# A new hand-written order of steps, with the same code

## The chip, the cores and the metric

The kernel runs on one core of a Trainium2 chip. The metric is the device time of one execution in microseconds. The core has five engines that run side by side, each with its own instruction stream in order: PE (TensorE: matmuls; its weight loads are listed as PEld), DVE (VectorE), ACT (ScalarE), POOL (GpSimd, which here mostly issues loads) and SP (SyncE, which here issues the writes of the result). They wait for one another by semaphores.

## The reference

```python
def _attn_ref(q, k, v, p):                       # q, k, v: 8 x 8 x 576 x 64, p: 8 x 8 x 32 x 64
    scale = 1.0 / np.sqrt(q.shape[-1])
    def sm_attn(qq, kk, vv):
        s = scale * np.matmul(qq, kk.transpose(0, 1, 3, 2))
        s = s - np.max(s, axis=-1, keepdims=True)
        a = np.exp(s)
        a = a / (np.sum(a, axis=-1, keepdims=True) + 1e-09)
        return np.matmul(a, vv)
    p_packed = sm_attn(p, k, v)
    return sm_attn(q, p_packed, p_packed)

# x: attention's output as 4608 tokens x 512;  w_in: 512 x 2048;  w_out: 2048 x 512
h = x @ w_in
r = np.maximum(h, 0.0)
out = (r * r) @ w_out
```

There are two attentions in a row: 32 packed rows attend to 576 keys, then 576 queries attend to the 32 results. After them comes a feed-forward layer with a squared relu.

## The kernel before

The work is cut by batch (8), by quad of four heads (2 in a batch), by half of a batch's 576 tokens (256 and 320 in batches 0 and 1, 288 and 288 after them), by block of 128 of the 2048 hidden columns (16, paired to 8), and by tile of 128 output rows (36). The second attention's product with `p_packed` isn't formed: `p_packed` is multiplied by w_in first (`wp`), so that layer 1 is the matmul of `wp` with the transposed weights `a2T`.

What runs when stands in one string, `ORDER`. Its words are steps, and `run` calls `step` for each in turn. Each step gives its instructions to one engine or two, so the words of one engine, in order, are that engine's instruction stream. A word's suffix names the engine where there is a choice: `:v` is DVE, `:a` is ACT, `:p` is POOL. A buffer is taken where the word that fills it stands, from those whose last reader stands earlier in the string.

The words, with batch b, quad n, half f, block i, pair j, tile t:

| words | step | engine |
|---|---|---|
| Lkbn, Lvbn, Lqb, LA/LB; Wi, Wo; Pr | loads of k, v, q (LA and LB are the parts of q of batches 0 and 1); of w_in and w_out in pieces; of the rest of p | POOL's queue |
| pf; P0, P1 | load of p of batches 0 and 1 (three DMAs into one tile); scaling and transposing it | SP; DVE |
| I | the identity matrix | POOL |
| Zn.m | n idle matmuls of 512 columns and m of 256 (L338); nobody uses their result | PE |
| kTbn; s1b; m1, x1 | transpose of k (L354); scores of the first attention; maximum, exponential | DVE; PE; DVE, ACT |
| eT, eo; pv, pp | transpose of the exponentials on PE and its copy; product with v and its scaling | PE, any; PE, DVE |
| pt, po; bd, bs | two transposes of pp and their copies | PE, any; DVE, any |
| QA, QB, EA, EB (batch 0); qA, qB, qT | transpose of q, on PE with a copy, or on DVE (L366) | PE, any; DVE |
| zA, zB, s2 | scores of the second attention (A and B are the halves in batches 0 and 1) | PE |
| t, m, s, x, u, a, T with A or B; t2, m2, sb, x2, su, a2, aT | softmax of it and the transpose to `a2T` | DVE, x on ACT, some on POOL |
| wa, wb, w0, w1; Wa, Wb, W0, W1 | `wp` in pieces of columns (L609); its copy out of PSUM (L452, L454) | PE; ACT or DVE |
| hb.f.i; rb.f.i; qb.f.j | layer 1 (L625); relu (L630 on ACT, L632 on DVE); square into `gT` (L668 on ACT, L670 on DVE) | PE; ACT or DVE; any |
| ot.j; ct; dt | two of a tile's 16 matmuls of layer 2 (L683); copy out of PSUM; write to DRAM (L714) | PE; ACT or DVE; SP |

PSUM holds two banks for tiles of `h` in batch 1 and after (`y`; in batch 0 two for even and two for odd blocks), two for tiles of `o` (`x`), and two double banks for the rest (`psa`). SBUF holds three buffers for k, two for q, three for v from batch 2 on, and five for a copied output tile (`o_sb`).

Of the kernel before, what the change touches and what calls it, by code (L numbers as in the profile page):

```python
# [70 lines left out]
qT21 q1.1.3:a o4.6 h1.1.12 r1.1.0:a bd2 pt2 qT20 o4.7 bs2:a Lk40 h1.1.5 po2:v r1.1.12:a o5.7 q1.1.0:v c4:a h1.1.10
r1.1.5:v c5:a s22 d4 r1.1.10:v h1.1.4 o6.0 t221 r1.1.4:a h1.1.9 d5 o7.0 q1.1.2:a t220 h1.1.13 r1.1.9:a o6.1 qT30
r1.1.13:a Lq4 h1.1.11 q1.1.4:a m221 w120 w121 r1.1.11:a o6.2 m220 W121:a h1.1.14 h1.1.15 W120:v Lv31 o6.3 r1.1.14:a
q1.1.6:a o7.1 o6.4 sb21:v r1.1.15:a Lv40 o7.2 q1.1.5:a kT30 o7.3 q1.1.7:a o7.4 sb20:v Lk41 x221 o6.5 qT31 o7.5 x220 o6.6
su21 o6.7 o7.6 su20 c6:a o7.7 w020 a221:v c7:a d6 w021 o8.0 W020:a a220:v o8.1 d7 o8.2 aT21 W021:a o8.3 aT20 o8.4 Lq5
h2.0.1 h2.0.0 r2.0.1:v o8.5 r2.0.0:a o8.6 q2.0.0:v h2.0.2 h2.0.3 r2.0.2:v o9.0 Lk50 o8.7 r2.0.3:v h2.0.5 c8:a s13
q2.0.1:v r2.0.5:a h2.0.4 d8 m130 o10.0 r2.0.4:a h2.0.6 kT40 h2.0.7 r2.0.6:a o10.1 r2.0.7:a q2.0.2:v h2.0.10 Lk51 x130
m131 o9.1 h2.0.8 r2.0.10:a q2.0.3:v o9.2 r2.0.8:a kT41 h2.0.13 x131 eT30 h2.0.9 r2.0.13:v o10.2 eo30:a rd3 r2.0.9:v
h2.1.1 eT31 q2.0.4:v h2.0.14 r2.1.1:a o10.3 r2.0.14:v eo31:a h2.0.11 Lk61 o9.3 r2.0.11:v o9.4 h2.0.12 h2.1.5 q2.0.5:v
r2.0.12:a pv3 r2.1.5:v h2.0.15 q2.0.6:v h2.1.4 pp3 r2.0.15:a o9.5 r2.1.4:v h2.1.6 bd3 pt3 q2.0.7:v h2.1.0 bs3:a o9.6  # L80
r2.1.6:v r2.1.0:v Lv41 po3:a o9.7 q2.1.2:v h2.1.8 q2.1.0:v c9:a h2.1.2 r2.1.8:v s23 r2.1.2:a Lv50 d9 o11.0 t230 h2.1.3
h2.1.7 t231 o10.4 r2.1.3:a w130 m230 r2.1.7:a w030 W130:a h2.1.10 q2.1.1:v h2.1.9 q2.1.3:v o10.5 W030:a m231 o10.6 o11.1
sb30:v r2.1.10:a o11.2 r2.1.9:a sb31:v o10.7 x230 o11.3 q2.1.4:v c10:a h2.1.15 qT40 o11.4 x231 h2.1.11 su30 r2.1.15:a
w031 d10 r2.1.11:a w131 W031:a h2.1.14 su31 h2.1.13 o12.0 r2.1.14:a a230:v o12.1 r2.1.13:a o12.2 W131:a q2.1.5:v o12.3
a231:v h2.1.12 o11.5 aT30 r2.1.12:a o12.4 aT31 o12.5 q2.1.6:v q2.1.7:v h3.0.5 h3.0.2 qT41 r3.0.5:a o12.6 h3.0.0 r3.0.2:v
Lq6 o11.6 r3.0.0:a o12.7 h3.0.1 h3.1.1 r3.0.1:v c12:a o11.7 r3.1.1:v s14 d12 c11:a q3.0.0:v h3.0.4 kT50 h3.0.3 r3.0.4:a
o13.0 r3.0.3:a m140 d11 h3.0.9 Lk60 o14.0 r3.0.9:a q3.0.1:v h3.1.3 x140 kT51 h3.1.0 o14.1 r3.1.3:a m141 o13.1 Lk70
r3.1.0:a h3.0.8 q3.0.2:v eT40 x141 h3.0.7 r3.0.8:v o13.2 eo40:v r3.0.7:a h3.0.6 q3.1.0:v o14.2 q3.0.4:v r3.0.6:a eT41
rd4 q3.0.3:v h3.0.11 eo41:a h3.1.2 r3.0.11:v o14.3 r3.1.2:v o13.3 h3.0.12 h3.0.10 q3.1.1:v pv4 r3.0.10:a r3.0.12:v o14.4
Lv51 pp4 h3.0.13 q3.0.5:v h3.0.14 r3.0.13:a bd4 o13.4 r3.0.14:v bs4:a pt4 Lv60 q3.0.6:v h3.0.15 h3.1.8 o13.5 po4:v  # L90
r3.1.8:a o14.5 r3.0.15:v s24 q3.0.7:v h3.1.11 t240 h3.1.6 r3.1.11:a o13.6 t241 r3.1.6:a o13.7 w040 qT51 c13:a w041
h3.1.4 W040:a m241 o16.0 d13 h3.1.5 m240 r3.1.4:a o16.1 r3.1.5:a o14.6 W041:a sb41:v h3.1.9 h3.1.7 q3.1.2:v o14.7
r3.1.7:a sb40:v r3.1.9:a w140 w141 x241 q3.1.3:v h3.1.10 c14:v o16.2 W141:a h3.1.13 q3.1.4:v d14 o15.0 su41 r3.1.10:a
o16.3 x240 o15.1 r3.1.13:v W140:a h3.1.12 q3.1.5:v o16.4 a241:v o15.2 r3.1.12:a h3.1.14 su40 h3.1.15 o16.5 r3.1.14:a
q3.1.6:v o15.3 r3.1.15:a a240:v o15.4 o16.6 q3.1.7:v o15.5 aT40 aT41 o16.7 qT50 o15.6 c16:a h4.0.1 h4.0.4 Lq7 r4.0.1:v
o15.7 d16 r4.0.4:v o17.0 c15:a h4.0.3 h4.0.2 r4.0.3:v o17.1 r4.0.2:a d15 s15 q4.0.1:v h4.0.0 kT60 h4.0.9 o17.2 r4.0.0:a
m151 o17.3 r4.0.9:a h4.0.6 m150 o17.4 r4.0.6:a h4.1.3 q4.0.0:v x151 o17.5 kT61 o18.0 x150 o17.6 r4.1.3:v Lk71 h4.0.5
h4.0.13 rd5 r4.0.5:a o18.1 r4.0.13:v eT50 h4.0.11 eo50:v h4.0.12 eT51 q4.0.2:v o17.7 r4.0.12:v r4.0.11:a o18.2 eo51:a
c17:v h4.1.2 h4.0.10 q4.0.6:v r4.1.2:a pv5 d17 r4.0.10:a h4.0.7 Lv61 q4.1.1:v h4.0.15 r4.0.7:a o19.0 q4.0.5:v r4.0.15:a
pp5 o19.1 q4.0.3:v o19.2 Lv71 bd5 h4.0.8 pt5 bs5:v h4.1.11 r4.0.8:a o18.3 po5:v q4.0.4:v h4.1.1 s25 r4.1.11:a r4.1.1:v  # L100
# [761 lines left out]
```

## Time and profile before

| | |
|---|---|
| time, median of 3 runs (lowest, highest) | 241.13 us (241.06, 241.85) |
| the profiled execution: its own time, its span | 242.64 us, 240.8 us |
| PE busy | 228.9 us, 95% of the span |
| DVE busy | 201.4 us, 84% |
| ACT busy | 144.2 us, 60% |
| POOL busy | 73.4 us, 30% |
| granted TensorE clock | 1.0 |

The span reaches from the first to the last instruction that was profiled; the execution's own time has the start and the end around it. A line of a group reads: line of the code, engine, operation, what it writes and reads, shapes, count, then busy time in us and the mean of one in ns, then the idle time of the engine just before. A line of the timeline reads: start and duration in us, engine, line, operation, tiles, shapes, count, and in brackets how long the engine stood idle before it and what ended that. A line of DMA issues ends with the size of one and the time from issue to landing. Some matmul records are missing from a trace.

### The profile page before, as it was taken

How to read it: one execution, taken by the hardware profiler on the slowest of the kernel's cores; microseconds unless marked ns; L12 is line 12 of the kernel's file. 1: busy time of each engine (PE TensorE's matmuls, PEld its weight loads, DVE VectorE, ACT ScalarE, POOL GpSimd, SP SyncE). 2: the span in 40 equal slices, each digit the busy share in tenths (PEclk: the TensorE clock that was granted, in tenths of full speed). 3: DMA queues.
4: the chain of work that ended last, by engine and by line, in shares of the span. 5: the costliest groups of instructions: out<-in, count | busy, mean ns of one | idle time of the engine just before them, and what ended most of it. 6: DMA issues, size and time to landing. Idle time of an engine off the chain costs nothing.

```text
span 240.8 us, 6042 instructions
## 1 busy us (share of the span) xinstructions
PE 228.9 (95%) x2373; PEld 124.6 (52%) x2408; DVE 201.4 (84%) x456; ACT 144.2 (60%) x311; POOL 73.4 (30%) x122
## 2 busy tenths in 40 slices
...
GB/s 108 177 197 209 187 197 206 172 239 195 197 194 211 177 169 144 44 78 211 110 79 37 196 125 52 59 37 102 39 23 73 49 46 44 44 41 49 46 63 112
DMA packets 33404, 28.51 MB, mean 118 GB/s; under 512 B 8160, under 2 KB 28384, under 8 KB 33376
## 3 DMA queue, kind: packets, MB, share of 16 engines
...
q1 hardware_dynamic: 6384, 9.51, 14.7%
...
## 4 chain that ended last, share of the span: by engine, by line
PE 83%; DVE 7%; DMA 4%; issue 2%; POOL 1%; SPq 1%; ACT 1%; POOLq 0%
PE ps_o L683 48%; PE ps_h L625 25%; DMA gT<-in_v_dram 4%; PE ps_wp L609 3%; PE ps_s L408 3%; PE ps_e1T L466 2%; PE ps_pv L490 1%; SPq L714 1%; DMA out_dram<-o_sb 1%; DVE gT L670 1%; DVE mx L558 1%; DVE d L564 1%; DVE r L632 1%; DVE sums L576 1%; ACT qT L452 1%
## 5 line engine op out<-in xcount | busy, mean ns | idle before, releaser
L683 PE MATMUL ps_o<-w_out_bf,gT 128*128 128x512 bf16 (+1 forms) x544 | 140.9, 378 | 2.0 <-issue 0.5
L625 PE MATMUL ps_h<-a2T,wp 128*128 128x288 bf16 (+2 forms) x512 | 89.9, 286 | 1.4 <-DVE wp L454 0.6
L630 ACT ACTIVATE r<-ps_h 128x288 bf16<-128x288 f32 (+2 forms) x161 | 61.4, 413 | 48.8 <-PE ps_h L625 43.2
L683 PEld LDWEIGHTS <-gT 128*128 128x128 bf16 x576 | 54.6, 98 | 43.6 <-issue 3.4
L625 PEld LDWEIGHTS <-wp 128*128 128x128 bf16 x512 | 47.4, 98 | 41.9 <-issue 7.4
L632 DVE TENSOR_SCALAR r<-ps_h 128x288 bf16<-128x288 f32 (+2 forms) x95 | 41.3, 449 | 11.3 <-PE ps_h L625 10.6
L670 DVE TENSOR_TENSOR gT<-r 128x576 bf16<-128x576 bf16 (+2 forms) x108 | 46.5, 444 | 2.1 <-ACT r L630 1.2
L452 ACT CAST wp<-ps_wp 128x1024 bf16<-128x1024 f32 (+1 forms) x31 | 29.1, 962 | 8.8 <-PE ps_wp L609 8.8
L452 ACT COPY o_sb<-ps_o 128x512 f32<-128x512 f32 x26 | 15.2, 590 | 12.3 <-PE ps_o L683 12.0
L271 POOL DMA_DIRECT2D q_b<-in_q_dram x16 | 11.0, 690 | 27.4 <-DVE qT L366 25.4
L271 POOL DMA_DIRECT2D k_b<-in_k_dram x28 | 15.2, 545 | 13.5 <-DVE kT L354 4.6
L316 POOL DMA_DIRECT2D v_b<-in_v_dram x12 | 9.3, 776 | 31.8 <-PE ps_pv L490 29.8
L446 ACT ACTIVATE e<-ps_s,nm 128x576 bf16<-128x576 f32 x16 | 11.8, 742 | 7.1 <-DVE nm L434 6.8
L354 DVE STREAM_TRANSPOSE kT<-k_b 128x576 uint32<-128x576 uint32 x16 | 12.3, 771 | 3.1 <-DMA k_b<-in_k_dram 3.1
L668 ACT ACTIVATE gT<-r 128x640 bf16<-128x640 bf16 (+1 forms) x18 | 12.2, 695 | 0.4 <-DVE r L632 0.3
L434 DVE TENSOR_REDUCE nm<-ps_s 128x1 f32<-128x576 f32 x16 | 11.5, 739 | 1.0 <-PE ps_s L408 0.9
L366 DVE STREAM_TRANSPOSE qT<-q_b 128x576 uint32<-128x576 uint32 (+2 forms) x16 | 10.8, 683 | 1.8 <-DMA q_b<-in_q_dram 1.8
L576 DVE TENSOR_REDUCE sums<-e 128x18 f32<-128x576 f32 (+2 forms) x20 | 12.1, 603 | 0.0
L570 ACT ACTIVATE e<-d 128x576 f32<-128x576 f32 (+2 forms) x20 | 11.7, 600 | 0.7 <-DVE d L564 0.6
L564 DVE TENSOR_TENSOR d<-s,mx 128x576 f32<-128x576 f32 (+2 forms) x19 | 11.7, 641 | 0.0
L558 DVE TENSOR_REDUCE mx<-s 128x18 f32<-128x576 f32 (+2 forms) x20 | 11.6, 609 | 0.0
L584 DVE TENSOR_TENSOR a<-e,rs 128x576 bf16<-128x576 f32 (+2 forms) x17 | 11.6, 708 | 0.0
...
## 6 DMA issues: line engine op xcount, KB each, us to landing
...
v_b<-in_v_dram POOLq DMA_DIRECT2D x12, 256.0 KB, 5.5
w_out_bf<-in_moe_w_out_dram POOLq DMA_DIRECT2D x4, 512.0 KB, 11.1
...
w_in_bf<-in_moe_w_in_dram POOLq DMA_DIRECT2D x4, 256.0 KB, 11.4
```

Source lines behind the costliest of these rows:

```text
L271: engine.dma_start(x[n:], s[:P - n])
L354: self.nc.vector.transpose(t["kT"][:].rearrange("p s e -> p (s e)").bitcast(U32), t["k"][:].rearrange("p t d -> p (t d)").bitcast(U32))
L452: engine.copy(out, x)
L558: self.nc.vector.tensor_reduce(out=mx[:, x], in_=t["s2"][:, x], op=ALU.max, axis=AX.X)
L564: engine.tensor_tensor(out=d2[:, x], in0=t["s2"][:, x], in1=t["mx"][:, x].unsqueeze(2).to_broadcast([P, n, NP]), op=ALU.subtract)
L576: nc.vector.reduce_sum(out=sums[:, x], in_=t["e2"][:, x], axis=AX.X)
L625: self.nc.tensor.matmul(ps, lhsT=t["wp"][:, fb // n, fb % n * P:(fb % n + 1) * P], rhs=t["a2T"][:, s0:s1], start=(qd == 0), stop=(qd == se ...
L630: engine.activation(r, ps, ACT.Relu)
L632: engine.tensor_scalar_max(r, ps, 0.0)
L668: engine.activation(out, r, ACT.Square)
L670: engine.tensor_tensor(out=out, in0=r, in1=r, op=ALU.mult)
L683: self.nc.tensor.matmul(self.o[tt][:, e], lhsT=self.gT[:, fb, a:a + P], rhs=self.w_out_bf[:, fb, e], start=(i == 0), stop=(i == self.NFB - 1))
```

## The change

The string `ORDER` is replaced as a whole; no other line of the program changes. The new string holds the same steps, apart from the idle matmuls: 29 of 512 columns and 5 of 256 before, 22 and 4 after. Steps that have a choice of engine are given out anew: of the squares 108 stand on DVE, 18 on ACT and 2 on POOL before, 59, 67 and 2 after. 161 relus stand on ACT before and 164 after. The copies of output tiles stay divided as they were (26 on ACT, 9 on DVE, the last on both).

The beginning, up to the first h steps that use the second half of `wp`:

```diff
-pf Lk00 P0 Lk01 kT00 Z14.0 s100 Lv00 LA0 kT01 m100 Z1.1 s101 m101 I x100 Lv01 x101 P1 Z2.1 eT00 LB0 eo00:v Z0.1 eT01
-QA01 QA00 eo01:v Wi11 EA00:a rd0 pv0 pp0 EA01:a Z1.0 pt0 Wi01 po0:v Z0.1 zA0 tA00 Wi00 tA01 mA00 Z1.0 QB01 QB00 EB00:a
-EB01:a mA01 sA00:v Wi10 Wi20 Z2.1 zB0 sA01:v xA00 xA01 tB00 Z5.0 wa01 tB01 wa00 Wi21 mB00 Wa01:a Z3.0 wb00 uA01 uA00
-mB01 sB00:p aA01:p xB00 Wa00:a TA01 sB01:v aA00:p TA00 Lk11 uB00 wb01 Wb00:a h0.0.8 h0.0.9 Lk10 h0.0.0 xB01 h0.0.1
...
-h0.1.0 r0.1.8:a w100 r0.1.3:a w101 r0.1.0:v h0.1.11 r0.1.1:a W101:a W100:v h0.1.2 Lv11 kT11 r0.1.2:a r0.1.11:a h0.0.5
...
+pf P1 Lk00 Lk01 I LA0 P0 kT00 Z14.0 s100 kT01 Lv00 s101 m100 x100 m101 QA00 Z2.0 eT00 Lv01 EA00:v x101 rd0 Z0.1 eT01 LB0
+Wi11 eo01:v eo00:a Wi00 Z0.1 pv0 pp0 Z1.0 pt0 Wi01 po0:v QA01 EA01:v zA0 QB00 tA00 Wi10 QB01 EB00:a Wi20 tA01 mA00 mA01
+EB01:a Wi21 sA00:v Lk11 sA01:v xA01 Z1.1 zB0 tB00 tB01 Z1.1 wa01 xA00 Wa01:a Lk10 mB00 wa00 uA00 uA01 sB00:p Z3.0 wb00
+aA00:p Wa00:a mB01 aA01:p TA00 sB01:v TA01 Wo0 xB00 Wb00:a h0.0.0 uB00 xB01 wb01 r0.0.0:v Wb01:a uB01 h0.0.9 h0.0.1 Lv11
...
+r0.1.1:a h0.1.0 w100 w101 h0.1.2 r0.1.0:v W100:v W101:a h0.1.11 h0.0.4 Lv10 r0.1.2:a r0.0.4:a h0.1.14 r0.1.11:v h0.1.15
...
```

The transposes of batch 1's q, the loads that follow, and batch 2's start:

```diff
-w111 qB10 w011 q0.0.7:a o3.2 o1.2 qB11 W011:a o0.2 q0.1.6:v o0.3 W111:a qA10 o2.2 zB1 qA11 tB10 zA1 tA11 tB11 o3.3 tA10
...
-r1.0.5:a o4.1 r1.0.7:v q1.0.2:a aB10:v h1.0.10 h1.0.8 q1.0.3:v r1.0.10:a o4.2 kT21 Lq2 h1.0.9 r1.0.8:a o5.2 r1.0.9:a
-h1.0.12 TB10 s12 q1.0.4:v r1.0.12:a h1.0.14 m120 o5.3 Lv30 r1.0.14:a h1.1.1 m121 h1.1.3 r1.1.1:a o5.4 x120 r1.1.3:v
...
+r0.0.15:v pv1 h0.1.5 Wo1 r0.1.12:a pp1 o3.0 q0.0.3:a q0.1.3:v r0.1.5:a pt1 po1:a qB10 o3.1 o1.0 q0.1.5:a o0.2 Wo3 o0.3
+Pr qB11 w111 w011 o2.2 bd1 qA11 W111:a W011:a qA10 o2.3 o1.1 q0.1.6:v o3.2 Lk21 zB1 zA1 tB10 o1.2 q0.1.2:a tB11 o3.3
...
+h1.0.3 o2.6 r1.0.3:a h1.0.9 h1.0.7 q1.0.0:v c3:a o2.7 Pu r1.0.9:a o4.0 r1.0.7:a h1.0.14 h1.0.15 q1.0.1:a Lq2 kT20 aB11:v
+r1.0.14:a s12 TB10 m120 r1.0.15:a c2:a h1.0.12 m121 r1.0.12:a h1.0.5 TB11 o4.1 r1.0.5:a o5.0 h1.0.4 h1.0.13 x120 o5.1
...
```

Places further on that the next section speaks of, and the end:

```diff
+rd2 o4.2 r1.1.4:a r1.0.10:v pv2 q1.0.5:v q1.0.4:a Lq5 pp2 qT21 h1.1.8 h1.1.7 q1.0.6:a o4.3 o4.4 r1.1.8:a r1.1.7:a bd2
...
+x130 r2.1.4:v d6 r2.0.8:v o8.2 o8.3 rd3 h2.0.7 h2.0.0 r2.0.7:a eT30 qT31 eT31 r2.0.0:v eo30:a eo31:v o7.7 q2.0.3:v
...
+h3.1.7 x241 o13.1 r3.1.7:v o13.2 h3.1.4 h3.0.15 d12 r3.1.4:a o14.4 o13.3 h3.1.13 su41 su40 r3.0.15:a o13.4 q3.0.7:v
+h3.1.14 o14.5 o14.6 r3.1.14:v o14.7 W040:a r3.1.13:a W140:a h3.1.8 Lv50 q3.1.2:a d2 r3.1.8:a h3.1.9 a240:v o13.5 a241:v
...
+h4.0.0 c15:a r4.0.3:a r4.0.0:a q4.0.1:v o16.4 h4.1.0 pt5 bd5 h4.0.12 o16.5 r4.1.0:a po5:a r4.0.12:v h4.0.10 q4.0.2:a
+bs5:a o17.0 h4.1.1 qT51 o17.1 s25 r4.1.1:v d13 r4.0.10:a q4.0.0:v h4.0.11 r4.0.11:a o16.6 q4.0.3:a t250 o17.2 h4.0.13
...
-h7.1.15 o33.4 r7.1.15:v o33.5 o33.6 q7.1.7:v o34.2 o34.3 o33.7 o34.4 c33:v o34.5 o34.6 o34.7 d33 o35.0 c34:v o35.1 o35.2
-d34 o35.3 o35.4 o35.5 o35.6 o35.7 c35 d35
...
+o34.3 d31 q7.1.6:a o33.6 o33.7 o34.4 o34.5 c33:v o34.6 o35.0 d32 o35.1 o34.7 o35.2 o35.3 o35.4 c34:a o35.5 d33 o35.6
+o35.7 c35 d34 d35
```

More of the change, by code (lines that the diff above doesn't have):

```diff
@@ L71 @@
[L71 to L100, printed above, removed]
@@ new lines @@
+m221 sb21:v o5.6 h1.1.9 o5.7 d1 sb20:v Lk31 r1.1.9:v o4.7 x221 w121 c5:a w120 o6.0 x220 q1.1.2:v c4:a h1.1.13 o6.1
+W121:a o7.0 r1.1.6:a su21 r1.1.13:a o7.1 o6.2 q1.1.3:a h1.1.14 h1.1.11 o7.2 su20 Lv31 a220:v o6.3 q1.1.4:a o7.3 a221:v
+r1.1.11:v h1.1.15 q1.1.5:a r1.1.15:a aT20 o6.4 o7.4 aT21 h2.0.10 Lv30 r1.1.14:v kT31 Lq3 h2.0.1 r2.0.10:v W120:a
+r2.0.1:a Lk50 kT30 o6.5 o7.5 h2.0.11 q1.1.6:v h2.0.2 s13 o6.6 r2.0.11:a r2.0.2:v h2.0.4 q1.1.7:a r2.0.4:a h2.0.5 o6.7
+q2.0.5:v kT41 Lk40 o7.6 h2.0.3 r2.0.5:a h2.0.6 c6:a q2.0.2:a m130 m131 r2.0.6:v o8.0 r2.0.3:a o8.1 h2.1.4 x131 h2.0.8
@@ new lines @@
+x130 r2.1.4:v d6 r2.0.8:v o8.2 o8.3 rd3 h2.0.7 h2.0.0 r2.0.7:a eT30 qT31 eT31 r2.0.0:v eo30:a eo31:v o7.7 q2.0.3:v
+h2.0.13 Lv40 h2.0.12 d3 r2.0.13:a pv3 kT40 pp3 r2.0.12:a o8.4 h2.1.9 r2.1.9:a q2.0.0:v bd3 qT30 h2.0.9 r2.0.9:a o8.5
+bs3:a pt3 po3:v h2.1.3 r2.1.3:v q2.0.1:a o8.6 c7:v d4 h2.0.15 r2.0.15:a o8.7 h2.1.8 c8:v s23 t230 q2.0.4:a t231 r2.1.8:a
+h2.0.14 r2.0.14:a o10.0 h2.1.1 m230 o9.0 m231 h2.1.5 o9.1 r2.1.1:a sb30:v Lq4 Lv41 r2.1.5:a h2.1.0 w131 r2.1.0:a w031
+h2.1.11 h2.1.2 q2.1.0:v W131:a o10.1 o9.2 o9.3 sb31:v o9.4 r2.1.2:a x230 r2.1.11:a q2.1.4:v h2.1.7 o10.2 q2.0.6:a su30
@@ new lines @@
+h2.1.12 x231 W031:a o10.3 r2.1.12:v o10.4 su31 o10.5 h2.1.13 r2.1.7:a w030 a230:v w130 r2.1.13:a q2.1.1:v q2.0.7:a
+W030:a W130:a aT30 h2.1.6 o10.6 r2.1.6:v h2.1.15 r2.1.15:a q2.1.3:v o10.7 o9.5 o9.6 a231:v h2.1.10 q2.1.6:v aT31
+r2.1.10:a o9.7 s14 q2.1.5:v h2.1.14 h3.0.2 c10:a o12.0 d8 qT40 c9:a q2.1.2:a o12.1 m140 m141 o11.0 r3.0.2:a o12.2
+r2.1.14:a h3.0.9 h3.1.2 x140 x141 d5 r3.0.9:v o12.3 r3.1.2:v o11.1 h3.0.1 eT40 r3.0.1:a h3.0.3 eT41 r3.0.3:a o12.4 Lk71
+h3.0.0 rd4 eo40:v eo41:a qT41 r3.0.0:v h3.0.4 o12.5 pv4 h3.0.7 q3.0.1:a r3.0.4:v q2.1.7:v pp4 bd4 r3.0.7:a h3.1.1 o11.2
@@ new lines @@
+pt4 po4:a h3.0.6 r3.1.1:v bs4:v r3.0.6:a o12.6 h3.0.5 s24 kT50 r3.0.5:v o12.7 h3.0.11 h3.0.10 q3.0.0:a d7 o11.3 o11.4
+r3.0.11:a h3.0.12 Lk51 t240 r3.0.10:a c12:a h3.1.3 q3.0.3:v r3.1.3:a r3.0.12:a t241 kT51 o14.0 q3.1.1:a o11.5 Lk61 m241
+h3.0.14 r3.0.14:a o11.6 m240 h3.0.8 o11.7 h3.0.13 o14.1 r3.0.8:a q3.0.2:v sb41:v r3.0.13:a q3.0.4:a h3.1.6 o14.2 h3.1.15
+w140 q3.0.6:v sb40:v r3.1.6:a r3.1.15:v w040 c11:a h3.1.5 o13.0 h3.1.0 o14.3 Lk60 x240 r3.1.5:v qT50 q3.0.5:a r3.1.0:v
+h3.1.7 x241 o13.1 r3.1.7:v o13.2 h3.1.4 h3.0.15 d12 r3.1.4:a o14.4 o13.3 h3.1.13 su41 su40 r3.0.15:a o13.4 q3.0.7:v
@@ new lines @@
+h3.1.14 o14.5 o14.6 r3.1.14:v o14.7 W040:a r3.1.13:a W140:a h3.1.8 Lv50 q3.1.2:a d2 r3.1.8:a h3.1.9 a240:v o13.5 a241:v
+o13.6 r3.1.9:v h3.1.11 w041 q3.1.0:a aT41 r3.1.11:v c14:a Lq6 w141 W041:a h3.1.12 h3.1.10 o15.0 aT40 o13.7 r3.1.10:v
+W141:a o15.1 h4.0.2 q3.1.3:v r3.1.12:a c13:v s15 q3.1.4:a o15.2 r4.0.2:v h4.0.6 o15.3 m150 r4.0.6:a o16.0 x150 h4.0.4
+r4.0.4:a d9 q3.1.6:a d11 q3.1.5:v o16.1 h4.0.5 Lv51 eT50 m151 kT61 h4.0.9 o15.4 r4.0.5:v r4.0.9:v x151 h4.0.1 o15.5
+q3.1.7:a eT51 r4.0.1:v h4.0.8 o16.2 eo50:v eo51:a h4.0.7 o15.6 o16.3 o15.7 kT60 r4.0.7:a h4.0.3 r4.0.8:a pv5 rd5 pp5
@@ new lines @@
+o17.7 d10 W151:v su50 x251 c17:a Lk70 r4.1.4:a h4.0.15 o18.5 s16 su51 o19.0 a250:v h4.1.14 r4.0.15:a a251:v aT50 m161
+q4.0.7:a o19.1 r4.1.14:a q4.1.5:a h4.1.13 o18.6 m160 h4.1.5 o19.2 o19.3 r4.1.13:a r4.1.5:a h4.1.6 aT51 o19.4 r4.1.6:a
+kT70 o18.7 x160 h5.0.11 h4.1.8 o19.5 r4.1.8:v q4.1.2:a o19.6 h4.1.12 o19.7 c18:a r5.0.11:v q4.1.3:a d15 r4.1.12:v c19:v
+eT60 h5.0.4 o21.0 o21.1 r5.0.4:v h5.0.9 x161 h5.0.1 qT60 o21.2 r5.0.9:v eT61 h5.0.0 o21.3 q4.1.6:v eo60:a r5.0.1:v
+h5.0.8 r5.0.0:v eo61:a o20.0 q4.1.4:a pv6 h5.0.5 r5.0.8:v h5.0.3 rd6 r5.0.5:a o20.1 pp6 o21.4 h5.0.6 d14 q5.0.4:v
@@ new lines @@
+r5.0.3:v pt6 kT71 r5.0.6:v h5.0.2 po6:v r5.0.2:a o20.2 o20.3 h5.0.14 q4.1.7:a r5.0.14:a h5.0.10 w060 w061 q5.0.2:v bd6
+h5.1.0 q5.0.0:a r5.0.10:v o20.4 W060:a r5.1.0:v h5.0.15 Lv71 r5.0.15:a q5.0.1:v bs6:a d18 o21.5 h5.1.5 W061:a o20.5
+o21.6 r5.1.5:v q5.0.7:a h5.0.13 h5.0.7 d17 o21.7 r5.0.7:a o20.6 s26 r5.0.13:v h5.1.1 c21:v t261 h5.1.6 o20.7 q5.0.5:a
+r5.1.6:a c20:a o22.0 r5.1.1:v o22.1 h5.1.3 o23.0 t260 h5.0.12 r5.1.3:a w160 w161 h5.1.11 r5.0.12:a h5.1.9 m261 W160:a
+m260 q5.0.3:v r5.1.11:v o22.2 q5.1.0:v sb61:v W161:a r5.1.9:a sb60:v o22.3 h5.1.2 o22.4 q5.0.6:a s17 h5.1.4 r5.1.2:v
@@ new lines @@
+o23.1 r5.1.4:a q5.1.1:v qT70 o23.2 x261 h5.1.14 r5.1.14:a o22.5 o23.3 o22.6 o23.4 o22.7 h5.1.7 m171 m170 x260 x170 su61
+Lv70 h5.1.10 o23.5 eT70 d16 r5.1.7:a su60 c22:a o23.6 h5.1.12 o23.7 r5.1.12:v o24.0 q5.1.2:a h5.1.13 r5.1.10:a q5.1.3:a
+d21 a260:v c23:a o24.1 a261:v aT60 r5.1.13:a h5.1.8 x171 r5.1.8:v o24.2 aT61 h5.1.15 r5.1.15:v o25.0 eo70:a eT71 o25.1
+q5.1.4:v h6.0.0 o24.3 o25.2 r6.0.0:v h6.0.5 h6.0.14 q5.1.6:v r6.0.14:v eo71:v q5.1.5:a o24.4 rd7 o24.5 h6.0.1 r6.0.5:a
+h6.0.6 r6.0.1:v r6.0.6:v qT71 pv7 pp7 q6.0.0:v o24.6 q5.1.7:a h6.0.11 bd7 d20 r6.0.11:a h6.0.10 o25.3 o24.7 h6.0.7 bs7:v
```

74 lines of the change are left out of this document (30 added, 44 removed).

## The prediction

> **What bounds the kernel now.** I read the page first, then busy time by stretch, then the waits of PE, then the timeline of the first 41 us with the landings of the loads.
>
> ```profile
> span 240.8 us, 6042 instructions
> PE 228.9 (95%) x2373; PEld 124.6 (52%) x2408; DVE 201.4 (84%) x456; ACT 144.2 (60%) x311; POOL 73.4 (30%) x122
> ...
> L670 DVE TENSOR_TENSOR gT<-r 128x576 bf16<-128x576 bf16 (+2 forms) x108 | 46.5, 444 | 2.1 <-ACT r L630 1.2
> ...
> L668 ACT ACTIVATE gT<-r 128x640 bf16<-128x640 bf16 (+1 forms) x18 | 12.2, 695 | 0.4 <-DVE r L632 0.3
> ```
>
> PE is busy 95% of the span. A square costs 444 ns on DVE and 695 ns on ACT. Its groups have 544 matmuls of L683 for 576 weight loads: 32 records are missing, and each leaves a false hole of 0.22 us.
>
> ```profile
> 0.00:21.60 21.60, 16.04 (x224) 7.73 (x228) 12.29 (x35) 8.19 (x16) 11.33 (x23) 1.00 1.11 168
> 21.60:41.00 19.40, 18.48 (x262) 10.60 (x263) 16.59 (x41) 15.79 (x37) 13.74 (x19) 1.00 1.21 198
> 41.00:229.50 188.50, 186.38 (x1849) 101.91 (x1868) 169.68 (x377) 119.91 (x258) 48.31 (x81) 1.00 0.62 107
> 229.50:241.00 11.50, 7.95 (x54) 4.38 (x51) 2.85 (x5) 0.27 (x1) 0.00 (x0) 1.00 0.30 77
> ```
>
> The columns are length, busy time of PE, PEld, DVE, ACT and POOL, granted clock, DMA share, GB/s. From 41 us to the tail PE lacks 2.1 us of 188.5, and most of that is missing records. What PE is said to wait for there:
>
> ```profile
> PE ps_o L683 <- issue: 0.5, 3, 0.2
> PE ps_o L683 <- DVE a2T L598: 0.2, 1, 0.2
> PE ps_o L683 <- DVE qT L366: 0.2, 1, 0.2
> ```
>
> That is 0.9 us in all. In the chain of waits twelve output matmuls take 2.60 us, 0.217 each, near the end as in the middle. So this stretch is a stream of matmuls with no room, and an order can shorten only what lies before it. There the landings rule (timeline, then answers on DMA for single issues):
>
> ```profile
> 5.94 0.78 DVE L354 STREAM_TRANSPOSE kT<-k_b 128x576 uint32<-128x576 uint32 x1 [2.43 <-DMA k_b<-in_k_dram]
> ...
> 13.17 0.36 PE L490 MATMUL ps_pv<-gT,e1T 96*32 96x64 bf16 x24 [0.54 <-DMA gT<-in_v_dram]
> ...
> 21.59 4.25 PE L625 MATMUL ps_h<-a2T,wp 128*128 128x256 bf16 x28 [0.44 <-DVE a2T L598]
> ...
> 25.77 0.63 PE L609 MATMUL ps_wp<-w_in_bf,ppT 64*32 64x512 bf16 x16
> ...
> 27.63 1.85 PE L625 MATMUL ps_h<-a2T,wp 128*128 128x256 bf16 x14 [0.58 <-DVE wp L454]
> ...
> 38.65 0.91 DVE L366 STREAM_TRANSPOSE qT<-q_b 128x320 uint32<-128x320 uint32 x2 [1.83 <-DMA q_b<-in_q_dram]
> ...
> 39.93 0.77 DVE L366 STREAM_TRANSPOSE qT<-q_b 128x256 uint32<-128x256 uint32 x2
> ...
> 40.09 1.07 PE L408 MATMUL ps_s<-qT,ppd 32*32 32x320 bf16 x32
> ```
> ```profile
> gT<-in_p_dram SPq DMA_DIRECT2D x1, 8.0 KB, 4.3
> ```
> ```profile
> w_in_bf<-in_moe_w_in_dram POOLq DMA_DIRECT2D x1, 512.0 KB, 13.7
> ```
> ```profile
> q_b<-in_q_dram POOLq DMA_DIRECT2D x1, 256.0 KB, 8.8
> ```
>
> Four landings set the pace: the second v at 13.13 (PE resumes at 13.17), the last piece of w_in at 25.7 (issued 11.96, plus 13.7; w100 starts at 25.77), and q of batch 1 in two pieces, at 38.6 and 39.9 (the second issued 31.09, plus 8.8). DVE waits 1.83 us for the first and stands ready for the second; PE has a short wait inside the 1.07 us at 40.09, whose 32 matmuls stream in about 0.8.
>
> **The change, part by part.** *Work.* I counted the words of both orders. Of the computing steps none is added or dropped. From DVE to ACT go 49 squares net, 3 relus, 2 copies of e1T and 2 of ppT; the two EA copies go from ACT to DVE. DVE: 49 x 0.444 + 3 x 0.449 + 2 x 0.48 + 2 x 0.28 - 2 x 0.42 (the nearest DVE copies of bf16 from PSUM take 0.48 for 640 columns and 0.28 for 256) = 23.9 us less, 177.5. ACT: 49 x 0.695 + 3 x 0.413 + 2 x 0.687 + 2 x 0.372 - 2 x 0.588 = 36.2 us more, 180.4. Both stay below PE's 229, and PE's real work is the same: 0 us by themselves. What hid them was PE's stream; without that cover one late square costs PE up to 0.70.
>
> *Fillers.* Idle matmuls fall from 29 full and 5 half ones to 22 and 4. At 0.216 a full one that is 1.6 us less PE work, all in waits before 21 us: 0 us, unless the clock falls (rival 1).
>
> *P1 ahead of P0.* P1 needs the last of the three SP loads of p, issued at 1.77 and landing 4.3 later, at 6.1; P0 needed only the first, at 2.98 on DVE. Behind P1 on DVE stand P0 and kT00. P1 6.14 to 6.64, P0 to 7.07, kT00 7.0 to 7.8 instead of 5.94 to 6.71: s100 is 1.05 us late. Who waits: m100 8.6, m101 9.3, x100 9.4, x101 10.25, QA00 (its q now loads ahead of v; in the trace the third load of the queue landed at 10.24) at 10.3, eT00 about 11.0, eT01 11.5, copies to 12.6. The second v lands at 13.13 as before, since the same bytes stand before it in POOL's queue. So the 1.05 us disappears behind that landing, with 0.5 to spare: 0, or +0.6 if q lands at 11.68 (its slot of before).
>
> *From pt0 to the first h.* QA01 now follows pt0, and EA01 sits on DVE after po0 (14.69), so zA0 comes at 15.3 instead of 14.75. QB then runs at 15.65 and 16.0, EB on ACT 16.05 to 17.35 as before, zB0 17.4 as before. DVE: tA, mA, sA by 17.86, tB to 18.7, mB00, uA00, uA01, mB01 to 20.46. POOL: sB00, aA00, aA01 to 21.03 (Lk11 and Lk10 are moved ahead of them, three issues of 0.57, done before 17). TA01 ends at 21.65: first h at 21.7, +0.1.
>
> *To w100 and zA1.* Both orders have the same 14 h steps between there and w100, and the same two between w101 and the first h that needs w's second half. ACT starts the relus at 22.85 instead of 22.29 (xB01 and Wb01 stand before them); with two PSUM banks per parity PE reaches w100 at 26.0 instead of 25.77, and h0.0.4 at 27.8 instead of 27.63: +0.15. Up to zA1 the orders hold the same PE steps but for one o step exchanged for another, and the loads stand in the same order up to q's second piece, so qA10 ends at 40.7 again. PE had about 0.27 of waiting there, which swallows the 0.15 to 0.25. Sum up to here: 0, bounds -0.1 and +0.6.
>
> *The stream after 41 us.* Same PE work. The order leaves more between an h and the h that takes its bank: the least is 0.80 of PE work in batches 2 to 7 instead of 0.68. Attention runs earlier. Three places are tighter. (a) kT20 has no PE step between its place and s12's. Its loads, now behind Lk21, land at about 50.8 by the issue slots of before (45.27 to 46.5, plus 4.1 to 5.1); kT20 ends at 51.6, PE reaches s12 at 52.4: no wait, +0.5 if they land late. (b) bs5 on ACT stands behind r4.1.0, po5 and a square: 1.08 + 0.4 + 0.3 + 0.65 + 0.6 = 3.05 after pv5, and PE has 3.05 of work up to s25: 0 to +0.4. (c) eT31 to pv3 has 0.9 of PE work for a DVE copy and its hand-over, about 0.75. The loads are issued in another order too (Lq5 before Lq3); the nearest, q of batch 2, has some 1.5 us to spare. Writes d are late on SP (d2 behind d12), yet of five o_sb buffers the wanted one is free at least 2 us ahead. I put the waits at 0.3 more than the 0.9 of now: bounds -0.9 and +1.5, taken nearest to the three rows above, none of which passes 0.2 a time.
>
> *Tail.* PE ends on the same o35, c35 and d35; d33 and d34 stand before. 3.3 us after the last matmul as now: 0.
>
> Sum: 0 + 0.3 = +0.3 on the profiled execution (its own time 242.64, its span 240.8), which is 1.5 above the median of the runs, 241.13. On the median: 241.4. A measurement of this kernel can tell about 0.3%, 0.72 us.
>
> **Rivals.** *1, slower: the clock.* The first 14 fillers start 0.43 us apart until 6.35, later ones 0.22: PE begins at half rate and needs 5.2 us of work to leave it. With eight fillers fewer and s100 late, PE has less work from 9 to 18 us; if it falls back, the h from 21.7 on run at half rate for up to 5.2 us and 2.6 us are lost, less 0.27: 243.5. For it: only continuous filling is shown to keep the rate. Against: the granted clock is 1.00 throughout, and the holes are about 1 us. [...] Chance 0.10.
>
> *2, slower: ACT becomes the late engine.* Place: bs and the eo copies before s2 and pv in batches 2 to 5, where PE has 2.0 to 3.1 us between pv and s2. It decides once ACT is a relu late there; 0.35 a batch, four batches: 242.5. For: ACT from 60% to 75%, squares 0.25 longer than DVE's. Against: DVE at 84% hid the like. Chance 0.27.
>
> *3, faster: the waits go.* All 0.9 after 41 us and the 0.27 vanish: 240.0. More isn't there, with PE's work unchanged. Chance 0.08, which includes a gap in this reading.
>
> **How the numbers follow.** The forecast has 0.55. Its own range is 240.5 to 242.2, of which nearly all lies within 0.3%. The whole range, 240.5 to 243.2, leaves out the low half of rival 3 and the clock's full price. Slower: 0.10 + 0.27; faster: 0.08.
>
> **What would show it.** First kT near 7.0, pv's second half at 13.2, first h near 21.7, h after w101 near 27.7, qT of batch 1 at 38.65; DVE near 177 us, ACT near 180; PE waits after 41 us near 1.2. Wrong if a landing among the four moves, if matmuls stand 0.43 apart after 21 us, or if PE waits for ACT L452 or L668.

## The result, and the profile after

The changed kernel takes 242.61 us (median of 6 runs, 242.16 to 242.90), the one before 241.32 (6 runs, 241.06 to 241.85). The ratio is 1.0049, 95% interval 1.0034 to 1.0064: slower by 1.3 us, more than the 0.3% that can be told from no change. It lies inside the forecast range of 240.5 to 243.2, but the forecast itself, the same at 241.4, did not come true.

The page of the profile after has these totals:

```profile
span 240.8 us, 6053 instructions
...
PE 227.9 (95%) x2363; PEld 124.1 (52%) x2400; DVE 182.3 (76%) x402; ACT 172.9 (72%) x365; POOL 73.3 (30%) x122
...
L668 ACT ACTIVATE gT<-r 128x576 bf16<-128x576 bf16 (+2 forms) x67 | 45.4, 688 | 1.5 <-DVE r L632 1.2
```

The span is 240.8 us, just as in the profile before. That is the first thing to explain, because the medians differ by 1.3. The profiled execution of before took 242.64, 1.3 above its kernel's median, and the one of after 242.66, which is its kernel's median.

The timeline answers step by step to the lines that the prediction showed:

```profile
6.76 0.73 DVE L354 STREAM_TRANSPOSE kT<-k_b 128x576 uint32<-128x576 uint32 x1
...
11.79 0.86 PE L490 MATMUL ps_pv<-gT,e1T 96*32 96x64 bf16 x48
...
20.21 0.49 PE L625 MATMUL ps_h<-a2T,wp 128*128 128x256 bf16 x2
...
24.84 0.98 PE L609 MATMUL ps_wp<-w_in_bf,ppT 64*32 64x512 bf16 x16
...
26.95 2.08 PE L625 MATMUL ps_h<-a2T,wp 128*128 128x256 bf16 x14 [0.48 <-DVE wp L454]
...
38.75 0.77 DVE L366 STREAM_TRANSPOSE qT<-q_b 128x256 uint32<-128x256 uint32 x2 [0.29 <-DMA q_b<-in_q_dram]
```

pv waits for no load (the second v landed at 12.01, not at 13.13), the first h stands at 20.21 instead of 21.59, w100 at 24.84 instead of 25.77 (all but its first matmul at 25.20, behind the last piece of w_in at 25.16), and the second part of batch 1's q is turned at 38.75 instead of 39.93. Every landing that the prediction had fixed came 0.5 to 1.2 us earlier, and yet nothing was won by the end.

What PE waits for from 41 us on is as small as it was:

```profile
PE ps_o L683 <- issue: 0.5, 3, 0.2
PE ps_o L683 <- DVE r L632: 0.2, 1, 0.2
PE ps_s L408 <- DVE qT L366: 0.2, 1, 0.2
```

That is 0.9 us, as before, with no wait on ACT's copies or squares. So the loss lies ahead of 41 us, and it shows only against an ordinary execution of the kernel before.

### The profile page after: what moved, and what is told of

Its sections match the earlier page's. It is cut to its first block, busy times and chain, and to the rows that moved or that the text cites. A ratio compares the mean times of both kernels' runs of the same rounds, so it can differ in the third digit from the quotient of the medians.

```text
span 240.8 us, 6053 instructions
## 1 busy us (share of the span) xinstructions
PE 227.9 (95%) x2363; PEld 124.1 (52%) x2400; DVE 182.3 (76%) x402; ACT 172.9 (72%) x365; POOL 73.3 (30%) x122
## 4 chain that ended last, share of the span: by engine, by line
PE 77%; DMA 9%; POOL 4%; DVE 4%; ACT 3%; issue 2%; DVEq 0%; POOLq 0%
PE ps_o L683 44%; PE ps_h L625 24%; DMA w_in_bf<-in_moe_w_in_dram 5%; DMA q_b<-in_q_dram 4%; PE ps_wp L609 3%; PE ps_s L408 2%; PE ps_e1T L466 1%; PE ps_pv L490 1%; POOL q_b L271 1%; DVE r L632 1%; POOL k_b L271 1%; ACT r L630 1%; POOL v_b L316 1%; DVE s L553 1%; ACT wp L452 1%
## 5 line engine op out<-in xcount | busy, mean ns | idle before, releaser
L630 ACT ACTIVATE r<-ps_h 128x288 bf16<-128x288 f32 (+2 forms) x164 | 63.0, 412 | 33.7 <-PE ps_h L625 32.1
L632 DVE TENSOR_SCALAR r<-ps_h 128x288 bf16<-128x288 f32 (+2 forms) x92 | 40.5, 450 | 27.0 <-PE ps_h L625 26.4
L668 ACT ACTIVATE gT<-r 128x576 bf16<-128x576 bf16 (+2 forms) x67 | 45.4, 688 | 1.5 <-DVE r L632 1.2
L670 DVE TENSOR_TENSOR gT<-r 128x576 bf16<-128x576 bf16 (+2 forms) x59 | 26.5, 458 | 2.1 <-ACT r L630 1.8
L271 POOL DMA_DIRECT2D k_b<-in_k_dram x28 | 15.2, 547 | 29.7 <-DVE kT L354 14.8
L609 PE MATMUL ps_wp<-w_in_bf,ppT 64*32 64x512 bf16 (+1 forms) x272 | 11.0, 369 | 1.6 <-DMA w_in_bf<-in_moe_w_in_dram 1.6
L273 POOL DMA_DIRECT2D k_b<-in_k_dram x19 | 10.0, 525 | 7.1 <-DMA q_b<-in_q_dram 5.1
```

The costliest lines, as they stand in the source:

```text
L271: engine.dma_start(x[n:], s[:P - n])
L609: self.nc.tensor.matmul(ps[NP * g:NP * g + NP, c, :f1 - f0], lhsT=t["ppT"][D * c:D * c + D, NP * h:NP * h + NP], rhs=self.w_in_bf[D * c:D ...
L630: engine.activation(r, ps, ACT.Relu)
L632: engine.tensor_scalar_max(r, ps, 0.0)
L668: engine.activation(out, r, ACT.Square)
L670: engine.tensor_tensor(out=out, in0=r, in1=r, op=ALU.mult)
```

## The experiments

The numbers of a run are medians. The kernel before ran beside each set and took 241.54 (34 runs), 241.49 (17) and 241.55 (30).

### The kernel before once more, and the two orders spliced

The program's text is the same but for the string. Three kernels take one order up to a word and the other order behind it (words already issued are not repeated):

```diff
 e2: new order up to zA1,  then the old one
 e3: old order up to zA1,  then the new one
 e4: new order up to w101, then the old one
```

> The kernel before, run and profiled once more. Its first profile was of an execution of 242.64 us, 1.3 above the median of its runs, and its loads landed later than those of the changed kernel though the queue held the same bytes (second piece of batch 1's q at 39.91 against 38.73). Theory A (the landings of that one execution were late, and the prediction took them for fixed): span 239.3 to 239.7, the second v at about 12.0 instead of 13.13, the last of w_in at 25.1 instead of 25.7, q at 38.7, and nearly no wait of PE at zA1. Theory B (the order of issue makes the landings): they land as in the first profile, span 240.8 or less only through shorter waits elsewhere.

241.57 (12 runs), ratio 0.9998 (0.9987 to 1.0009). Its profiled execution took 241.66, with a span of 239.8:

```profile
6.11 0.78 DVE L354 STREAM_TRANSPOSE kT<-k_b 128x576 uint32<-128x576 uint32 x1 [2.61 <-DMA k_b<-in_k_dram]
...
24.86 0.96 PE L609 MATMUL ps_wp<-w_in_bf,ppT 64*32 64x512 bf16 x16
```

In this execution the second v landed at 12.08 (13.13 in the profile that I predicted from), the last piece of w_in at 25.15 (25.70), and batch 1's q at 37.33 and 38.61 (38.62 and 39.91); w100 ran at 24.86, h0.0.5 at 26.95. The old order follows its loads when they come early, and PE waits there for almost none of them. This is the execution to compare with.

> The new order up to zA1 (about 40 us), then the old order with what is left. Theory 1 (the loss lies in the opening: PE waits for ACT at 21.4, 0.59 us, and for the exponential of batch 1 at 31.5, 0.47 us): 242.3 to 242.7, ratio 1.004 to 1.006. Theory 2 (the loss lies in the stream after zA1: s22 at 60.6, 0.32, and smaller ones): 241.2 to 241.6, ratio within 0.1% of 1.

242.61 (11 runs), 1.0059 (1.0038 to 1.0079): the whole loss is there with the old order from zA1 on. Five of its eleven executions had a mean granted clock of 0.984 to 0.993; the other six have a median of 242.40. Its profile, of the execution at 0.984, shows the clock falling twice:

```profile
6.50:9.90 3.40, 1.67 (x50) 1.05 (x48) 2.94 (x7) 0.00 (x0) 2.06 (x4) 1.00 1.24 190
9.90:13.40 3.50, 3.50 (x56) 2.49 (x44) 1.67 (x5) 2.46 (x5) 1.58 (x3) 0.51 1.28 199
20.20:23.60 3.40, 1.83 (x27) 1.11 (x20) 3.30 (x11) 2.50 (x7) 3.38 (x6) 0.99 1.23 208
23.60:27.00 3.40, 3.40 (x17) 2.12 (x15) 2.16 (x7) 2.55 (x8) 2.63 (x4) 0.50 1.15 207
```

The number behind a stretch and its length is PE's busy time, and the third from the end the granted clock.

> The old order up to zA1, then the new order with what is left: the mirror of the run before. Theory 1: 241.2 to 241.7, ratio up to 1.0015. Theory 2: 242.3 to 242.7, ratio 1.004 to 1.006. If both halves lose, the two ratios less 1 add up to 0.005.

241.93 (12 runs), 1.0018 (1.0003 to 1.0034). The new stream behind an old opening costs 0.4 us, give or take as much. Its profile shows one short PE hole, 0.13 us ahead of s12 where kT20 is late: place (a) of the prediction.

> The new order up to w101 (about 25 us), then the old order with what is left. If the loss of the opening lies ahead of w101 (P1 first, EA on DVE, fewer idle matmuls, relus held up behind Wb01): as e2, 242.3 or more. If it lies between w101 and zA1 (ACT late for batch 1's exponential): 241.2 to 241.6. Theory 2: 241.3 as well.

241.77 (12 runs), 1.0007 (0.9994 to 1.0021), with six executions at a clock of 0.993; the other six have a median of 241.68. So most of the loss, 0.7 of 0.9 us at full clock, falls between w101 (25 us) and zA1 (40 us), a stretch that the prediction had set to 0.

### The square beside GpSimd's square

Between those marks the timeline of the changed kernel shows a late step:

```profile
28.68 1.25 POOL L670 TENSOR_TENSOR gT<-r 128x640 bf16<-128x640 bf16 x1 [0.16 <-ACT r L630]
28.87 1.74 DVE L670 TENSOR_TENSOR gT<-r 128x640 bf16<-128x640 bf16 x2
30.54 1.41 DVE L434 TENSOR_REDUCE nm<-ps_s 128x1 f32<-128x576 f32 x2
...
31.31 0.74 ACT L446 ACTIVATE e<-ps_s,nm 128x576 bf16<-128x576 f32 x1 [0.50 <-DVE nm L434]
...
32.19 0.54 PE L466 MATMUL ps_e1T<-ident,e 128*96 128x128 bf16 x6 [0.31 <-ACT e L446]
```

The same steps in the kernel before (its second profile):

```profile
29.16 1.29 POOL L670 TENSOR_TENSOR gT<-r 128x640 bf16<-128x640 bf16 x1 [1.96 <-ACT gT L668]
29.60 1.42 DVE L434 TENSOR_REDUCE nm<-ps_s 128x1 f32<-128x576 f32 x2 [0.26 <-PE ps_s L408]
...
31.53 0.50 PE L466 MATMUL ps_e1T<-ident,e 128*96 128x128 bf16 x6
```

Read it from below: PE waits for the exponential, ACT waits 0.50 us for the maximum, and the maximum stands behind two squares that take 1.74 us together; the first alone takes 1.41, where one of its size takes 0.45 (28.18 in the first profile of the kernel before). They run while GpSimd makes a square of its own. So I moved one of them behind the maxima (e5), put the old fillers back (e6), and did both (e7); e8 is e4 with the old fillers.

```diff
 e5:
-r0.0.14:a s11 h0.0.7 q0.0.2:v LA1 h0.1.4 q0.1.4:p h0.1.13 h0.0.6 m111 q0.1.7:p r0.0.7:a m110 r0.1.4:a
+r0.0.14:a s11 h0.0.7 LA1 h0.1.4 q0.1.4:p h0.1.13 h0.0.6 m111 q0.1.7:p r0.0.7:a m110 q0.0.2:v r0.1.4:a
 e6 (ahead of the steps named):
+Z1.1 s101   Z2.1 eT00 (was Z2.0)   Z0.1 zA0   Z1.0 QB01   Z2.1 zB0 (was Z1.1)   Z5.0 wa01 (was Z1.1)
```

> The new order with one word moved: VectorE's square q0.0.2 goes behind batch 1's two row maxima m111 and m110 instead of ahead of them. In the changed kernel's profile that square took 1.41 us (28.87 to 30.28) beside GpSimd's square of 28.68 to 29.93, where VectorE's squares take 0.41 to 0.45 otherwise, and the maximum behind it began at 30.54 though its scores were out by 29.6. Theory 1 (the square is held until GpSimd's ends, and that makes the transposes eT11 late): the maximum begins near 29.6, the exponential near 30.8 instead of 31.31, the hole of 0.47 to 0.6 us ahead of eT11 goes, the kernel ends 0.4 to 0.6 us earlier: near 242.1, +0.2% on before. Theory 2 (the loss of the opening is the clock's, or is spread over many waits): less than 0.2 us of change, 242.5 or more.

242.73 (6 runs), 1.0058 (1.0040 to 1.0076): no gain (the two executions at full clock took 242.59, against 242.56 for the five of the changed kernel). I had taken the wrong one of the two squares. The long one has 640 elements, which is q0.1.1; q0.0.2 has 512 and takes 0.41.

> The new order with the fillers of the old one put back at the same steps: 7 of 512 columns and 3 of 256 more, some 1.8 us of TensorE work ahead of 18 us. Theory 1 (the missing fillers leave the clock to fall in some executions, and where it does not fall they cost nothing): no execution has a mean granted clock of 0.993 or less, where 5 of 11 and 6 of 12 had in the two kernels with the new opening; the median stays within 0.3 us of the changed kernel's 242.6 or comes below it, since most of its own executions had 0.998 or more. Theory 2 (the fillers were on the path, and fewer of them were a gain): the median rises by up to 1 us, to 243 or more. Theory 3 (the clock falls for another reason than the missing fillers): executions at 0.993 are still there.

242.41 (6 runs), 1.0039 (1.0026 to 1.0052). By count it has 7 full and 2 half fillers more, not 3 half ones. Five of six executions are at full clock and lie at 242.28 to 242.78, the sixth (0.993) at 244.89; in that one, which was profiled, the loads landed late as well (p's third part at 7.33, the second piece of batch 1's q at 40.67). The fillers cost nothing that can be seen, and do not make the fall impossible.

> Both edits at once on the new order: the square behind the maxima and the fillers back. If the two causes are separate, the gains add: 0.4 to 0.6 us from the square, 0 to 0.3 from the clock, so 241.8 to 242.2, with no execution at 0.993, and what is left against before (0.2 to 0.6 us) is the stream after 41 us. If the clock is not the fillers', executions at 0.993 remain and it comes out as the square alone.

242.86 (6 runs), 1.0057 (1.0040 to 1.0073). Its profile, at a clock of 0.998, has eT11 at 31.65 with no hole ahead of it. The lost time came back behind it:

```profile
32.38 0.76 PE L625 MATMUL ps_h<-a2T,wp 128*128 128x256 bf16 x4 [0.19 <-DVE r L632]
...
33.64 0.59 PE L683 MATMUL ps_o<-w_out_bf,gT 128*128 128x512 bf16 x2 [0.17 <-DVE r L632]
```

PE now waits for relus on VectorE. Its queue has no gap longer than 0.11 us from 26.7 to 34.4 us, so a square put behind the maxima delays the relus instead.

> The new order up to w101 (24.9 us), the old one behind it, and the old order's fillers put back. The same without the fillers gave 241.77 with 6 of 12 executions at a clock of 0.993, and a profile whose span of 239.5 us was 0.3 us under that of the kernel before. Theory 1 (the new opening itself is no worse, its missing fillers are): no execution at 0.993, median 241.3 to 241.6, at or a little under before. Theory 2 (the fillers delay the opening by what they take): 242 or more. Theory 3 (the fall has another cause): executions at 0.993 remain and the median stays near 241.8.

242.07 (12 runs), 1.0022 (1.0007 to 1.0037), two executions at 0.991: not the gain that I expected. The ten at full clock have a median of 242.00, where e4's six have 241.68, so theory 2, that the fillers delay this opening, is not excluded.

### P1, and the clock

In the profiles with the new opening PE stands still ahead of the first scores, for 0.76 us in the changed kernel, 2.07 in e5, 2.56 in e6. The cause is P1: p's third part lands between 5.6 and 6.4 us (in e6 at 7.3, with k's first half at 7.2), and with P1 first in VectorE's queue P0 and the turn of k wait for it. Four kernels take this apart: P1 in front in the old order (e9), P1 behind EA00 in the new one (e10), the same with GpSimd's second square issued later (e11), and e4 with P1 behind (e12).

```diff
 e9:
-pf Lk00 P0 Lk01 kT00 Z14.0 s100 Lv00 LA0 kT01 m100 Z1.1 s101 m101 I x100 Lv01 x101 P1 Z2.1 eT00
+pf P1 Lk00 P0 Lk01 kT00 Z14.0 s100 Lv00 LA0 kT01 m100 Z1.1 s101 m101 I x100 Lv01 x101 Z2.1 eT00
 e10, e11, e12:
-pf P1 Lk00 Lk01 I LA0 P0 kT00 Z14.0 s100 kT01 Lv00 s101 m100 x100 m101 QA00 Z2.0 eT00 Lv01 EA00:v x101
+pf Lk00 Lk01 I LA0 P0 kT00 Z14.0 s100 kT01 Lv00 s101 m100 x100 m101 QA00 Z2.0 eT00 Lv01 EA00:v P1 x101
 e11 as well: q0.1.7:p not behind m111 but behind Wo3
```

> The old order with one word moved: P1 (VectorE's cast and turn of p for batch 1) at the head of its queue, as the new order has it, ahead of P0 and the first turn of k. In the runs so far p's third part, which P1 reads, lands at 5.8 to 6.3 us, P0's at 3.5 to 4.5, and k's first half at 5.7 to 6.4; with P1 in front the first turn of k began at 6.76 to 7.47 and the first scores at 7.55 to 8.26, without it at 5.94 to 6.11 and 6.77 to 7.08, and TensorE had stood still for 0.8 to 2.6 us ahead of them, where the old order had 0.35. Theory 1 (P1's place alone lets the clock fall and delays the opening): some executions have a mean granted clock of 0.993 or less, where the old order has had none in more than 60, and the median rises by 0.2 to 0.8 us, to 241.7 to 242.3. Theory 2 (P1 lies in the shadow of later landings, as I had predicted; the clock and the delay come from other steps of the new opening): 241.4 to 241.6, no execution at 0.993.

242.07 (12 runs), 1.0016 (0.9996 to 1.0037). Nine executions at full clock have a median of 241.68, three at 0.991 take 243.12 to 243.33. The timeline of one of the three:

```profile
6.10 0.49 DVE L234 TENSOR_SCALAR p_b<-gT 128x128 bf16<-128x128 f32 x1 [4.54 <-DMA gT<-in_p_dram]
...
7.47 1.40 DVE L354 STREAM_TRANSPOSE kT<-k_b 128x576 uint32<-128x576 uint32 x2
...
8.26 1.02 PE L408 MATMUL ps_s<-kT,pT 32*32 32x192 bf16 x24 [1.99 <-DVE kT L354]
```

k had landed at 5.77; its turn starts at 7.47, and PE has idled for 1.99 us. From 8.45 us on the granted clock is one half for 3.4 us.

> The new order with that word taken back from the front: P1 behind the copy EA00, where VectorE stood idle for 0.57 us in the changed kernel (10.52 to 11.09). Theory 1: the first scores begin near 7.0, no execution is at 0.993 or less (after, and the three kernels that share its opening without more fillers: 16 of 35), and the median comes down by 0.3 to 0.6 us, to 242.0 to 242.3. Theory 2 (P1 hidden, something else lets the clock fall): 242.5 to 242.7, some executions at 0.993.

242.79 (12 runs), 1.0050 (1.0029 to 1.0071): a miss as a whole, since eight executions are at 0.993 or less, more than with P1 in front. The four at full clock lie at 242.04 to 242.32, with a median 0.4 under that of the changed kernel's five (242.16 to 242.90). Where the clock falls now is seen in the profile's stretches and in PE's waits just ahead of the fall:

```profile
13.00:16.40 3.40, 2.48 (x51) 1.58 (x52) 2.65 (x9) 1.29 (x2) 1.06 (x3) 1.00 1.44 199
16.40:19.80 3.40, 1.71 (x29) 0.52 (x21) 3.33 (x11) 1.32 (x4) 1.93 (x4) 0.98 1.37 200
19.80:23.20 3.40, 3.40 (x28) 1.67 (x28) 2.94 (x10) 3.33 (x8) 3.03 (x5) 0.51 1.24 207
```
```profile
17.93 0.28 PE L609 MATMUL ps_wp<-w_in_bf,ppT 64*32 64x256 bf16 x1 [1.06 <-DMA w_in_bf<-in_moe_w_in_dram]
...
18.84 0.41 PE L609 MATMUL ps_wp<-w_in_bf,ppT 64*32 64x256 bf16 x15 [0.63 <-DMA w_in_bf<-in_moe_w_in_dram]
```

PE works 1.71 of 3.4 us while wa01 and wa00 wait for w_in, and in the next 3.4 us it gets half the clock, just where layer 1 begins. The old order has Z5.0 at that place, the new one Z1.1.

> The same, and GpSimd's second square q0.1.7 issued later, behind its loads Wo1 and Wo3, so that it runs near 30 to 31.3 us and not beside VectorE's square q0.1.1, which took 1.33 to 1.41 us beside it in the profiles of the changed kernel and of the kernel with q0.0.2 moved (0.41 otherwise). Moving q0.0.2 did not help there: the square that was held was the other one, and the 0.6 us between o2.1 and o0.0 stayed. Theory 1 (the held square delays everything behind it on VectorE, which has no gap from 27 to 34 us): q0.1.1 takes 0.45, the maxima begin 0.6 to 0.9 earlier, no hole at eT11 nor at the layer 1 steps behind it, 0.4 to 0.7 us less than with P1 back alone: 241.5 to 241.9. Theory 2 (VectorE's queue is late there for what the new order puts on it, not for the collision): within 0.2 us of the run with P1 back alone.

243.22 (7 runs), 1.0054 (1.0031 to 1.0076), six of seven at 0.993 or less, so the time says little; the seventh took 243.06. The profile decides nothing either: q0.1.1 took 1.22 us again, this time beside GpSimd's two issues of w_out.

```profile
28.75 1.55 POOL L264 DMA_DIRECT2D w_out_bf<-in_moe_w_out_dram  x2
29.07 1.56 DVE L670 TENSOR_TENSOR gT<-r 128x640 bf16<-128x640 bf16 x2
```

> A version made of both: the new order up to w101 with P1 behind EA00, the old order from there on. With P1 in front it gave 241.77 and 6 of 12 executions at 0.993, and a profile at full clock that was 0.3 us shorter than that of the kernel before. Theory 1 (the new opening without P1 in front is the better one): no execution at 0.993 and 241.1 to 241.4, under before's 241.5. Theory 2 (all openings end at the last landing of w_in and batch 1's loads): 241.4 to 241.6, as before. If executions at 0.993 remain, something beside P1 and the fillers lets the clock fall.

241.93 (11 runs), 1.0014 (0.9998 to 1.0030); eight executions at 0.993 or less, the other three at 241.34, 241.41 and 242.15. It is no faster than the kernel before, so no version here beats it.

The executions of all kernels, sorted by P1's place and by the fillers ahead of 21 us (0.993 or less counts as a fall):

| P1 | fillers | kernels | executions | with a fall |
|---|---|---|---|---|
| behind | old | before (81), e1, e3 | 105 | 1 |
| in front | old | e6, e7, e8, e9 | 36 | 7 |
| behind | fewer | e10, e11, e12 | 30 | 22 |
| in front | fewer | after, e2, e4, e5 | 35 | 16 |

P1 in front is enough by itself to let the clock fall: e9 differs from before in that word alone and fell in 3 of 12. For the fillers this is not shown by themselves, since e10 to e12 have the rest of the new opening too. With P1 in front, putting them back took the falls from 16 of 35 to 4 of 24 (e6, e7, e8). With P1 in front the opening runs later against the same landings, so that the hole ahead of wa01 is shorter (0.68 us in the changed kernel's profile, 1.06 in e10's), which fits that the last row has fewer falls than the third. What a fall costs differs (median of the executions with one against that at full clock): 0.3 us in e4, 0.7 in e12, 1.5 in e9, where it comes together with late first scores; two of them took an execution of e2 to 244.97, against 242.40. Why e4 pays so little is not shown, as none of its falls was profiled.

## Why the prediction was right and wrong

**The baseline.** It was the first wrong step: one profiled execution, known to be 1.5 us above the median, was taken for the kernel's course, and its four landings for fixed points. The surplus was called outside the sum, but it was inside: it was the late landings, behind which the opening's own delays were hidden. Against the second profile of before, the lateness of the same PE work (a step's start less the stream time of the PE steps ahead of it, o 0.43, h 0.22 and 0.27, fillers left out) grows like this from before to after: 0 at h0.0.4 (27 us), 0.1 at o2.1 (31), 0.7 at o0.0 (33), 0.8 at o0.3 (38), 1.0 at the end.

**From w101 to zA1, set to 0.** Here lay 0.8 of the 1.0 between the two profiles. The count of PE steps was right, but the queue of VectorE was not followed: batch 1's maxima stand behind two squares, one of which is held to 1.41 us, and eT11 comes 0.66 us later than before. "PE had about 0.27 of waiting there, which swallows" it was true of the late execution only. By the rows, the held square takes 0.96 more than its like, and without that the maximum could begin near 29.6, as in before: an estimate. The same sum over all profiles fits: from h0.0.4 to h0.1.12 the lateness grows by 0.8 to 1.0 us in the seven kernels with the new order there (the square took 1.41 in the changed kernel, 1.33 in e7 and 1.22 in e11), and not at all in the six with the old order there. But no run freed the square in the new order (e5 and e7 moved the other one, and e11 did not free it), so how much is the square's and how much comes from the order of VectorE's words stays open.

**P1 ahead of P0, +1.05 and hidden.** The first scores came 0.5 us later in the profile (7.55 against 7.08) and 1.2 us in others, and pv ended at 12.65, against 12.70 before. So it was hidden, but not behind the landing that was to hide it: the second v came at 12.01, and pv's second half waited for a copy of e1T that ended at 12.23, against 12.10 before. What I missed is what PE does meanwhile: it stands still (1.99 us in e9's profile), and with P1's place as the only change the clock fell in 3 of 12 executions (e9).

**First h, w100, h0.0.4.** Forecast 0.1 to 0.2 later than before. Measured (the first h, w100, the first h with w's second half) at 20.21, 24.84 and 26.95, against 20.68, 24.86 and 26.95: 0.5 earlier, then even. The last pieces of w_in set w100 in both, as the prediction said.

**Fillers, 0 "unless the clock falls" (rival 1, 0.10, 243.5).** The condition is met far more often than 0.10 where the fillers are missing, 38 of 65 executions. The reason against it, that the holes are about 1 us, was no reason: in e10 the clock fell behind a stretch of 3.4 us with holes of 1.06 and 0.63. The length, 5.2 us, was read off the start of one execution (where the spacing of 0.43 ends at 5.86 already, not at 6.35); every fall in the profiles lasts 3.4, and the price of 2.6 is above that of one fall in the medians. Yet rival 1 isn't why the median rose: of the changed kernel's six executions one fell, at 242.66, and the five others have a median of 242.56. In e2 the two falls begin 13.7 us apart, four times the 3.4 that each lasts. PE was not idle ahead of them: it was busy for 1.67 and 1.83 of the 3.4 us before e2's two falls, and for 1.71 before e10's. Counted in steps of 3.4 us from the edges of the granted clock, the stretches ahead of all nine falls in the profiles had 0.90 to 2.13 us of work, while stretches with 1.79 (e7), 1.85 (e8) and 1.97 (the changed kernel, 16.34 to 19.75) passed without one: here busy time tells where the risk lies, and no sharp limit.

**The engine move and rival 2 (0.27, 242.5).** DVE fell by 19.1 us to 182.3 and ACT rose by 28.7 to 172.9, where the sum had 23.9 and 36.2. The squares on ACT took 688 ns, as priced, and ACT's groups added up rise by 36.1; the page's total counts the time in which two instructions overlap only once, which the sum left out. No PE wait on ACT's squares or copies after 41 us: rival 2 did not come.

**The stream, +0.3.** e3 says 0.4 with an interval from 0.1 to 0.8; the lateness above grows by 0.2 from o0.3 to the end. Right in size. **The tail, 0.** Right: 1.0 late at o35.7, 1.0 late at the end.

So most of the 1.3 us is the opening's, 0.7 of it between 31 and 38 us at full clock; the chance of 0.37 for slower stood on two other mechanisms. That 242.61 lies inside the whole range is luck: its upper end was put there for the two rivals, and neither of them raised the median.
